# A fused attention and mixture-of-experts kernel: its general path moved into loops

## The chip, the cores and the metric

The kernel runs on one core of one Trainium2 chip. The metric is device time in microseconds, the median over runs. A profile is one execution, recorded by the hardware profiler; its span runs from the first to the last instruction.

## The reference

Two blocks follow each other. The first is attention with 8 batches, 8 heads, 576 positions and 64 values for each head, with a window of 128 positions and a bias that falls with distance. Its output is laid out as 4608 tokens of 512 values. The second sends each token to one of 8 experts:

```python
scores = np.where(mask, scale * (q @ k.T) + bias, -1e9)   # 0 <= i - j < 128
x = (softmax(scores) @ v)                                 # -> (4608, 512)
logits = x @ w_gate
expert_idx = np.argmax(logits, axis=1)
gate_w = softmax(logits)[np.arange(N), expert_idx]
for e in range(8):                                        # the tokens of expert e
    y[e's tokens] = np.maximum(x[e's tokens] @ w1[e], 0) @ w2[e]
out = gate_w[:, None] * y
```

The inputs are small random numbers (normal, times 0.1 or less).

## The kernel before

**Attention.** The 4608 tokens are 36 tiles of 128. A loop that is written out in full runs over 32 units, each two heads of one batch. For each unit TensorE forms scores (L639), ScalarE their exponentials (L646), VectorE multiplies with a table of distance factors (L652), and TensorE multiplies with the values (L672). This form takes no maximum before the exponential, so it is only right where the sums of exponentials stay in range.

**Routing.** While that runs, the logits of each tile give every token an expert and a slot. GpSimd scatters the rows of `x` to `x_rows`, a tensor in HBM with a region for each expert, with one indirect DMA for each tile (`scatter`, which calls `to_x_rows`, L135). `clear` writes rows of zeros behind an expert's last token with further indirect DMAs.

**Experts.** `experts(True)` takes each expert's first 512 rows in one full group, by seven products in place of eight (`seven1`, `seven2`, L1048), and between the full groups seven single tiles of 128 for what overflows the 512. `send_out` (L465) scatters each tile of results to the output with an indirect DMA on GpSimd. The order of instructions on each engine is the order of the text: the whole stretch stands under `tc.manual_schedule()`.

**The general path.** Three things can break the fast path: sums of exponentials out of range, more than seven overflowing tiles, and fewer than 256 early rows for the first expert. `count_in_range` and `what_is_left` count them on VectorE, behind the expert with index 1, into `n_more`. At the end one register tells whether any of them happened:

```python
    with tc.If(more[0] == 0, label="nothing", preferred_fallthrough_block=False) as nothing:
        pass
    with nothing.Else():
        n_bad = nc.values_load(n_more_i[0:1, 1:2], ...)
        with tc.If(n_bad > 0):
            n_pass[0] = 1
            shifted()
            clear(free_rows[:, 0, :])
            with moe_pools(), tc.manual_schedule():
                experts(False)
```

`shifted()` is attention once more, tile by tile and with a maximum; `experts(False)` is the whole of the experts once more, written out. Below it stand a short group for the early rows and a loop over further overflowing tiles. With the inputs here none of the three happens, and the branch "nothing" is taken.

**Semaphores across a branch.** Instructions signal semaphores that only count up, and later waits are for fixed counts. A branch that skips code therefore has to raise each semaphore by what the skipped code would have added. For the engines and for SP's DMAs this is one semaphore instruction each. For GpSimd's own DMAs, which take turns on eight semaphores DMASW0 to DMASW7 and add 16 each, it is one instruction with eight amounts, INC_SWDGE_SEM. These instructions stand in the block "nothing" and carry the line of the outer `tc.If` (L1268). The end of the program, with a DRAIN on each engine and barriers among all of them, carries the line that opens the tile context (L1316).

Of the kernel before, what the change touches and what calls it, by code (L numbers as in the profile page):

```python
# [8 lines left out]
F32 = mybir.dt.float32  # L9
# [6 lines left out]
P = 128  # L16
# [5 lines left out]
def kernel(  # L22
# [92 lines left out]
    RW = Dm + 2  # L115
    x_d = nc.dram_tensor("x_rows", (E * N, RW), F32, kind="Internal").ap()
    zero_row = consts.tile([P, RW], F32, name="zero_row")
    soon.append(lambda: nc.gpsimd.memset(zero_row[:], 0.0))
# [15 lines left out]
    def to_x_rows(row, numbers, apart=True):  # L134
        ins = nc.gpsimd.indirect_dma_start(  # L135
            out=x_d[:, :], out_offset=bass.IndirectOffsetOnAxis(ap=numbers, axis=0),
            in_=row, in_offset=None, bounds_check=E * N - 1, oob_is_err=False,
        )
        ins = getattr(ins, "ins", ins)
        if apart:  # L140
            tc.declare_no_dep(ins, group=f"rows_in{n_pass[0]}", reason="disjoint rows")
            tc.add_to_no_dep_group(f"rows_in{n_pass[0]}", ins)

# [11 lines left out]
    n_routed = [0]  # L155
    n_pass = [0]

# [96 lines left out]
    def shifted():  # L254
        with tc.tile_pool(name="bias", bufs=1) as b_pool, \
# [44 lines left out]
            for t in range(NT):  # L300
# [79 lines left out]
                nc.vector.tensor_scalar_add(gw[:], gw[:], 1e-9)  # L380
                if t == NT - 1:
                    number_all_free(rows)
                xs = rows.tile([P, RW], F32, name="xs")
                nc.scalar.copy(xs[:, :Dm], xf)
                nc.vector.tensor_copy(xs.bitcast(I32)[:, Dm : Dm + 1], tok_i[:, t : t + 1])
                nc.vector.reciprocal(xs[:, Dm + 1 :], gw[:])
                scatter(t, xs[:])

    xe = rte.tile([1, NX], I32, name="xe")
    n_more = rte.tile([1, 4], F32, name="n_more")
    n_more_i = rte.tile([1, 4], I32, name="n_more_i")
    xr = rte.tile([1, NX], I32, name="xr")
    xmasks = rte.tile([P, 2, NX], I32, name="xmasks")

    def extras(scr):
        used = [0]

        def part(rows, n, m=None):  # L400
# [3 lines left out]
            return t if m is None else t.rearrange("p (a b) -> p a b", b=m)  # L404


        def to_masks(out, has):
            nc.vector.tensor_scalar_mul(out[:, 0], has, -1.0)
            nc.vector.tensor_scalar(
                out[:, 1], has, scalar1=-float(2 * N), scalar2=float(2 * N), op0=ALU.mult, op1=ALU.add,  # L410
            )

# [51 lines left out]
    def send_out(g, j, row):  # L464
        ins = nc.gpsimd.indirect_dma_start(  # L465
            out=out[:, :], out_offset=bass.IndirectOffsetOnAxis(ap=g["si"][:, j : j + 1], axis=0),
            in_=row, in_offset=None, bounds_check=N - 1, oob_is_err=False,
        )
        ins = getattr(ins, "ins", ins)
        if g["apart"]:  # L470

            tc.declare_no_dep(ins, group=f"rows_out{n_pass[0]}", reason="disjoint rows")
            tc.add_to_no_dep_group(f"rows_out{n_pass[0]}", ins)

# [486 lines left out]

    def what_is_left(first):
        if first:
            gps = pools["ps"].tile([P, DB * P], F32, name="tp")
            nc.tensor.matmul(gps[:, 0:1], lhsT=ones_sq[:], rhs=n_in[:], start=True, stop=True)
            nc.vector.tensor_scalar(
                n_more[:, 1:2], gps[0:1, 0:1], scalar1=-1.0, scalar2=float(N * H), op0=ALU.mult, op1=ALU.add,
            )

            nc.vector.tensor_scalar(  # L970
                n_more[:, 3:4], early_n[0:1, :], scalar1=-1.0, scalar2=float(EJ * P), op0=ALU.mult, op1=ALU.add,
            )
            nc.vector.tensor_scalar_max(n_more[:, 3:4], n_more[:, 3:4], 0.0)

            nc.vector.tensor_scalar(
                n_more[:, 2:3], n_more[:, 0:1], scalar1=-float(XU), scalar2=0.0, op0=ALU.add, op1=ALU.max,
            )
            nc.vector.tensor_add(n_more[:, 2:3], n_more[:, 2:3], n_more[:, 1:2])
            nc.vector.tensor_add(n_more[:, 2:3], n_more[:, 2:3], n_more[:, 3:4])
        else:  # L980
            nc.vector.memset(n_more[:, 1:], 0.0)
        nc.vector.tensor_copy(n_more_i[:], n_more[:])
# [178 lines left out]

    def of_x(x):
        ex = nc.sync.value_load(xe[0:1, x], min_val=0, max_val=E - 1)
        return (
            moe_w1[bass.ds(ex, 1)].rearrange("e d f -> (e d) f"), moe_w2[bass.ds(ex, 1)].rearrange("e f d -> (e f) d"),
        )

    def rows_of_x(x):
        r0 = nc.sync.value_load(xr[0:1, x], min_val=0, max_val=E * N - P)
        return x_d[bass.ds(r0, P), :]  # L1170

    def get_w1(g):
        g["src"] = of_x(g["x"]) if "x" in g else (moe_w1[g["e"]], moe_w2[g["e"]])
        g["w1"] = load_w1(g["src"][0])
# [4 lines left out]

    def experts(first):  # L1180
        groups = []
        for e in range(E):

            j0 = EJ if first and e == 0 else 0
            groups.append(dict(
                n=NJ - j0, e=e, rows=lambda r=e * N + j0 * P, n=NJ - j0: x_d[r : r + n * P, :], apart=True,
            ))
            if e > 0:
                x = slice(e - 1, e)
                groups.append(dict(n=1, x=x, rows=lambda x=x: rows_of_x(x), mask=xmasks[:, :, x], apart=True))  # L1190
        g = groups[0]
        if first:
            g["w1"], g["w2"] = expert_w.pop(0)
        else:
            get_w1(g)
        gather(g)
        get_w1(groups[1])
        gather(groups[1])
        if not first:
            g["w2"] = load_w2(g["src"][1])  # L1200
            extras(pools["wk"].tile([P, FB, NJ * P], F32, name="h_sb").rearrange("p f n -> p (f n)"))
            run(w1_sums(g))
        turns = [lambda: turn(g, range(g["n"])), lambda: tokens(g)]
        if first:
            zx = pools["u"].tile([P, Dm], F32, name="zx", bufs=1)
            layer2(early, EJ - 1, bank(2), zx[:], between=turns)
        else:
            run(turns)
            x_sums(g)
        for i, g in enumerate(groups):  # L1210
# [6 lines left out]
            if g["n"] == NJ:  # L1217
                hidden(g)
                order = (1, 6, 7, 5, 2, 3, 4)
                ws = w2_sums(g)  # L1220
                seven1(g, 0, order, two_banks(3), temps(), {6: ws[:1], 7: ws[1:2], 5: ws[2:3], 3: ws[3:]})
                if i == 1:
                    what_is_left(first)
                seven1(g, 1, order, two_banks(3), temps(), {})
            else:
                if i == 0:
                    run(w1_sums(full[0]))
                for fb in range(FB):
                    layer1(g, fb, bank(fb))
            if after[1] is not None:  # L1230
                get_w1(after[1])
            if after[0] is not None:
                turn(after[0], range(after[0]["n"]))
                tokens(after[0])
                if after[0]["n"] == NJ:
                    x_sums(after[0])
            if i == 0 and first:
                count_in_range()
            if g["n"] == NJ:
                g["zo"] = pools["wk"].tile([P, NJ, Dm], F32, name="zo")  # L1240

                ws = w1_sums(full[0]) if full else []
                seven2(g, {5: ws[:1], 2: ws[1:2], 3: ws[2:3], 4: ws[3:]})
            else:
                plain_layer2(g, ahead=[is_there_more] if first and i == len(groups) - 1 else ())

# [5 lines left out]
    with moe_pools():  # L1252
        tc.mark_branch_hint_location("nothing", engines=mybir.ALL_ENGINES)
        experts(True)
    order_all.close()

    def plain_group(g):
# [7 lines left out]
        plain_layer2(g)  # L1265


    with tc.If(more[0] == 0, label="nothing", preferred_fallthrough_block=False) as nothing:  # L1268
        pass
    with nothing.Else():  # L1270
        n_bad = nc.values_load(n_more_i[0:1, 1:2], min_val=0, max_val=N * H)
        with tc.If(n_bad > 0):
            n_pass[0] = 1
            shifted()
            clear(free_rows[:, 0, :])
            with moe_pools(), tc.manual_schedule():
                experts(False)

        n_short = nc.values_load(n_more_i[0:1, 3:4], min_val=0, max_val=EJ * P)
        with tc.If(n_short > 0):  # L1280
            with moe_pools():
                plain_group(dict(n=EJ, e=0, rows=lambda: x_d[: EJ * P, :], apart=False))

        nx = nc.values_load(n_more_i[0:1, 0:1], min_val=0, max_val=NX)
        with tc.If(nx > XU):
            with moe_pools(), tc.For_i(XU, nx, 1) as i:
                mk = pools["u"].tile([P, 2, 1], I32, name="mk")
                nc.vector.tensor_copy(mk[:], xmasks[:, :, bass.ds(i, 1)])
                x = bass.ds(i, 1)
                plain_group(dict(n=1, x=x, rows=lambda: rows_of_x(x), mask=mk, apart=False))  # L1290

# [28 lines left out]
```

## Time and profile before

| | |
|---|---|
| median of 4 runs | 724.0 us |
| lowest and highest run | 722.19 and 726.42 us |
| profiled execution | 723.61 us, span 721.8 us |
| mean granted TensorE clock | 0.989 |
| instructions in the span | 13669 |
| GpSimd's indirect DMAs in the span | 107 (68 to `x_rows`, 39 to the output) |
| last matmul ends | about 706 us after the start |

Idle time of an engine that is not the bottleneck costs nothing. In the profile an engine's name with a q behind it is its sequencer, which reads instructions, branches and waits for semaphores; such instructions are not counted as busy. The length given for a DMA that GpSimd issues is the time GpSimd spends on it, not the time until its data has landed.

### The profile page before, as it was taken

How to read it: one execution, taken by the hardware profiler on the slowest of the kernel's cores; microseconds unless marked ns; L12 is line 12 of the kernel's file. 1: busy time of each engine (PE TensorE's matmuls, PEld its weight loads, DVE VectorE, ACT ScalarE, POOL GpSimd, SP SyncE). 2: the span in 40 equal slices, each digit the busy share in tenths (PEclk: the TensorE clock that was granted, in tenths of full speed). 3: DMA queues.
4: the chain of work that ended last, by engine and by line, in shares of the span. 5: the costliest groups of instructions: out<-in, count | busy, mean ns of one | idle time of the engine just before them, and what ended most of it. 6: DMA issues, size and time to landing. Idle time of an engine off the chain costs nothing.

```text
span 721.8 us, 13669 instructions
## 1 busy us (share of the span) xinstructions
PE 687.9 (95%) x5662; PEld 560.4 (78%) x5662; DVE 345.4 (48%) x705; ACT 215.6 (30%) x543; POOL 120.0 (17%) x146
## 2 busy tenths in 40 slices
PE   6999999999899999999999999999999999999991
PEld 5777677766676688878897887889788888978880
DVE  4577666675763354426335533634562463435300
ACT  5655455554411121222131212112121221212120
POOL 1011322023343020121022002202200220200020
PEclk9999999999999999999999999999999999999996
DMA  9966789852226736265353617534362735371010
GB/s 268 272 207 191 237 273 297 232 169 75 90 90 210 269 88 233 68 231 175 132 186 140 238 56 280 189 132 164 140 197 111 282 120 202 99 273 51 1 60 4
DMA packets 52722, 121.49 MB, mean 168 GB/s; under 512 B 7185, under 2 KB 7185, under 8 KB 52656
## 3 DMA queue, kind: packets, MB, share of 16 engines
q1 hardware_dynamic: 43568, 101.50, 43.0%
q0 software_dynamic: 8560, 19.06, 7.2%
q8 instruction: 45, 0.74, 0.4%
q14 instruction: 21, 0.17, 0.1%
q10 hardware_dynamic: 528, 0.02, 0.0%
HBM read 101.51 MB, written 28.12 MB: 180 GB/s over the span
## 4 chain that ended last, share of the span: by engine, by line
PE 82%; issue 11%; DVE 3%; POOL 1%; DMA 1%; ACT 0%; SPq 0%; POOLq 0%; DVEq 0%
PE b L1048 17%; PE a L1048 11%; PE c L1048 11%; PE sp L639 7%; PE m L672 7%; PE a L517 6%; PE sm L693 3%; PE b L506 3%; PE a L506 3%; PE m L804 2%; PE m L506 2%; PE c L506 2%; PE tp L497 1%; PE m L753 1%; PE c L517 1%
## 5 line engine op out<-in xcount | busy, mean ns | idle before, releaser
L465 POOL DMA_INDIRECT out_dram<-zo,si x28 | 29.6, 1059 | 292.8 <-ACT zo L1118 288.5
L646 ACT ACTIVATE e<-sp 128x384 f32<-128x384 f32 x128 | 55.7, 492 | 52.1 <-PE sp L639 24.0
L639 PE MATMUL sp<-q_sb,k_sb 64*64 64x192 f32 (+2 forms) x1152 | 58.8, 325 | 9.5 <-DMA k_sb<-in_kT_dram 5.4
L672 PE MATMUL m<-probs,v_sb 64*64 64x192 f32 (+2 forms) x1152 | 62.6, 316 | 5.3 <-issue 3.5
L672 PEld LDWEIGHTS m<-probs,v_sb 64*64 64x64 f32 x1152 | 53.3, 135 | 14.6 <-issue 8.2
L639 PEld LDWEIGHTS sp<-q_sb,k_sb 64*64 64x64 f32 x1152 | 47.8, 138 | 21.0 <-issue 10.1
L517 PE MATMUL a<-w,h 128*128 128x512 f32 x128 | 56.3, 592 | 0.0
L1118 ACT ACTIVATE zo<-zo,gw 128x256 f32<-128x256 f32 x42 | 19.1, 502 | 119.4 <-DVE zo L1129 78.2
L1048 PE MATMUL a<-xgT,w 128*128 128x256 f32 x224 | 53.0, 379 | 0.0
L1048 PE MATMUL b<-xTs,w1s 128*128 128x256 f32 x224 | 52.9, 379 | 0.0
L1048 PE MATMUL a<-w,h_sb 128*128 128x256 f32 x224 | 50.6, 379 | 0.0
L1048 PE MATMUL b<-w2s,hs 128*128 128x256 f32 x224 | 50.6, 379 | 0.0
L1048 PEld LDWEIGHTS a<-xgT,w 128*128 128x128 f32 x224 | 42.5, 190 | 8.7 <-issue 3.3
L1048 PEld LDWEIGHTS b<-xTs,w1s 128*128 128x128 f32 x224 | 42.6, 190 | 5.8
L1048 PEld LDWEIGHTS b<-w2s,hs 128*128 128x128 f32 x224 | 42.6, 190 | 5.8
L1048 PEld LDWEIGHTS a<-w,h_sb 128*128 128x128 f32 x224 | 42.0, 190 | 5.4
L652 DVE TENSOR_TENSOR probs<-e,fac 128x1152 f32<-128x1152 f32 x32 | 43.3, 1352 | 3.0 <-ACT e L646 3.0
L517 PEld LDWEIGHTS a<-w,h 128*128 128x128 f32 x128 | 23.7, 190 | 26.8 <-issue 26.8
L135 POOL DMA_INDIRECT x_rows<-xs,slots x36 | 38.0, 1055 | 15.2 <-POOL xs L820 6.4
L1078 DVE TENSOR_TENSOR u<-b,p 128x512 f32<-128x512 f32 x14 | 9.7, 692 | 56.6 <-PE b L1048 28.7
L1082 ACT ACTIVATE h_sb<-h_sb 128x512 f32<-128x512 f32 x14 | 8.8, 631 | 84.3 <-DVE h_sb L1081 84.3
L681 DVE TENSOR_TENSOR xT<-xT,m 128x128 f32<-128x128 f32 x32 | 9.1, 284 | 51.1 <-ACT xT L680 51.1
(246 smaller groups left out, 1152.0 us busy)
## 6 DMA issues: line engine op xcount, KB each, us to landing
w<-in_moe_w_dram SPq DMA_DIRECT2D x28, 2048.0 KB
q_sb<-in_qT_dram SPq DMA_DIRECT2D x32, 288.0 KB
k_sb<-in_kT_dram SPq DMA_DIRECT2D x32, 288.0 KB
xg<-x_rows SPq DMA_DIRECT2D x16, 514.0 KB
v_sb<-in_v_dram SPq DMA_DIRECT2D x24, 256.0 KB
w<-in_moe_w_dram SPq DMA_DIRECT2D x8, 512.0 KB
v_sb<-in_v_dram SPq DMA_DIRECT2D x24, 128.0 KB
xg<-x_rows SPq DMA_DIRECT2D x7, 257.0 KB
```

What stands on the lines that cost most here:

```text
L135: ins = nc.gpsimd.indirect_dma_start(out=x_d[:, :], out_offset=bass.IndirectOffsetOnAxis(ap=numbers, axis=0), in_=row, in_offset=None, bou ...
L465: ins = nc.gpsimd.indirect_dma_start(out=out[:, :], out_offset=bass.IndirectOffsetOnAxis(ap=g["si"][:, j : j + 1], axis=0), in_=row, in_of ...
L506: nc.tensor.matmul(ps[:, :n], lhsT=g["w1"][:, db, fb * P : (fb + 1) * P], rhs=g["xT"][:, db, :n], start=(db == 0), stop=(db == DB - 1),)
L517: nc.tensor.matmul(ps[:], lhsT=g["h"][:, fb, j * P : (j + 1) * P], rhs=g["w2"][:, fb, :], start=(fb == 0), stop=(fb == FB - 1),)
L639: nc.tensor.matmul(sp_banks[2 * par + s][r * HALF : (r + 1) * HALF, c : c + n], lhsT=k_sb[u][head, k0 : k0 + HALF], rhs=q_sb[u][head, q0 : ...
L646: nc.scalar.activation(exps[u][:, c], sp_banks[s][:, : W // 2], AF.Exp, scale=D ** -0.5)
L652: nc.vector.tensor_tensor(to[:, :, : 3 * C].rearrange("p a (j c) -> p a j c", c=C), e[:, :, : 3 * C].rearrange("p a (j c) -> p a j c", c=C ...
L672: nc.tensor.matmul(xp[r][par * HALF : (par + 1) * HALF, q0 : q0 + n], lhsT=v_sb[b][keys, i, h * D : (h + 1) * D], rhs=probs[u][keys, par, ...
L693: nc.tensor.matmul(sm[g : g + 32, i * HALF : i * HALF + C], lhsT=one_c[:, hp, :], rhs=probs[u][:, par, c : c + C], start=(hp == 0 and i == ...
L804: nc.tensor.transpose(m[:, 2 * hp : 2 * hp + 2, :].rearrange("p h d -> p (h d)"), xT[pair][:, hp, c : c + P], ident[:],)
L1048: nc.tensor.matmul(out_of[:, i, :], lhsT=lhs(i, k), rhs=rhs(k), start=(first and i == 0 and k == 0), stop=(k == nk - 1), skip_group_check= ...
L1118: nc.scalar.activation(o[:, th, dh, i, :], src[:, i, :], AF.Copy, scale=g["gw"][:, j : j + 1])
```

## The change

In the general path, `shifted()` no longer scatters its 36 tiles of rows with 36 indirect DMAs that are written out. It stores each tile to a new tensor `x_by_token` with a plain DMA, and a loop then loads tile after tile and scatters it with the one indirect DMA in its body. `experts(False)` is gone: a second loop takes the 32 tiles (8 experts of 4) one by one, with masks in place of rows of zeros. The loop over overflowing tiles is shared as `one_tile`; its first index becomes a fifth value in `n_more`. `experts` loses its argument, and the groups of declared independence their pass number.

```diff
+    x_tok = nc.dram_tensor("x_by_token", (NT, P, RW), F32, kind="Internal").ap()
...
@@ shifted
-                if t == NT - 1:
-                    number_all_free(rows)
...
-                scatter(t, xs[:])
+                nc.sync.dma_start(x_tok[t], xs[:])
...
-    n_more = rte.tile([1, 4], F32, name="n_more")
-    n_more_i = rte.tile([1, 4], I32, name="n_more_i")
+    n_more = rte.tile([1, 5], F32, name="n_more")
+    n_more_i = rte.tile([1, 5], I32, name="n_more_i")
...
@@ what_is_left
+        nc.vector.memset(n_more[:, 4:5], float(XU))
...
+    def one_tile(i, of, first_row, masks):
+        mk = pools["u"].tile([P, 2, 1], I32, name="mk")
+        nc.vector.tensor_copy(mk[:], masks[:, :, bass.ds(i, 1)])
+        x = bass.ds(i, 1)
+        plain_group(dict(
+            n=1, of=lambda: of_x(x, of), rows=lambda: rows_of_x(x, first_row), mask=mk, apart=False,
+        ))
+
+    def all_again():
+        shifted()
+        with tc.tile_pool(name="again", bufs=1) as again:
+            with tc.For_i(0, NT, 1) as i:
+                xs = again.tile([P, RW], F32, name="xs")
+                sl = again.tile([P, 1], I32, name="sl")
+                nc.sync.dma_start(xs[:], x_tok[bass.ds(i, 1)].rearrange("o p r -> (o p) r"))
+                nc.vector.tensor_copy(sl[:], slots[:, bass.ds(i, 1)])
+                to_x_rows(xs[:], sl[:], False)
+            extras(again.tile([P, FB * NJ * P], F32, name="scr"))
...
+            with moe_pools(), tc.For_i(0, E * NJ, 1) as i:
+                one_tile(i, fe.rearrange("o e j -> o (e j)"), fr.rearrange("o e j -> o (e j)"), fmasks)
...
+        nc.vector.memset(n_more[:, 1:], 0.0)
+        nc.vector.tensor_copy(n_more_i[:], n_more[:])
...
         with tc.If(n_bad > 0):
-            n_pass[0] = 1
-            shifted()
-            clear(free_rows[:, 0, :])
-            with moe_pools(), tc.manual_schedule():
-                experts(False)
+            all_again()
...
+        x0 = nc.values_load(n_more_i[0:1, 4:5], min_val=0, max_val=XU)
         nx = nc.values_load(n_more_i[0:1, 0:1], min_val=0, max_val=NX)
-        with tc.If(nx > XU):
-            with moe_pools(), tc.For_i(XU, nx, 1) as i:
-                ...
+        with tc.If(nx > x0):
+            with moe_pools(), tc.For_i(x0, nx, 1) as i:
+                one_tile(i, xe, xr, xmasks)
```

More of the change, by code (lines that the diff above doesn't have):

```diff
@@ L140, in to_x_rows @@
         if apart:
-            tc.declare_no_dep(ins, group=f"rows_in{n_pass[0]}", reason="disjoint rows")
-            tc.add_to_no_dep_group(f"rows_in{n_pass[0]}", ins)
+            tc.declare_no_dep(ins, group="rows_in", reason="disjoint rows")
+            tc.add_to_no_dep_group("rows_in", ins)
     def clear(rows, apart=True):
@@ L155 @@
     n_routed = [0]
-    n_pass = [0]
     early_end = (NB - 2) * S // P
@@ L386, in shifted, with to_masks @@
                 nc.vector.reciprocal(xs[:, Dm + 1 :], gw[:])
-                scatter(t, xs[:])
+                nc.sync.dma_start(x_tok[t], xs[:])
     xe = rte.tile([1, NX], I32, name="xe")
-    n_more = rte.tile([1, 4], F32, name="n_more")
-    n_more_i = rte.tile([1, 4], I32, name="n_more_i")
+    n_more = rte.tile([1, 5], F32, name="n_more")
+    n_more_i = rte.tile([1, 5], I32, name="n_more_i")
     xr = rte.tile([1, NX], I32, name="xr")
     xmasks = rte.tile([P, 2, NX], I32, name="xmasks")
+    def to_masks(out, has):
+        nc.vector.tensor_scalar_mul(out[:, 0], has, -1.0)
+        nc.vector.tensor_scalar(
+            out[:, 1], has, scalar1=-float(2 * N), scalar2=float(2 * N), op0=ALU.mult, op1=ALU.add,
+        )
     def extras(scr):
@@ L404, in part @@
             return t if m is None else t.rearrange("p (a b) -> p a b", b=m)
[L407 to L411, printed above, removed]
         og = part(P, E, NX)
@@ L470, in send_out @@
         if g["apart"]:
-            tc.declare_no_dep(ins, group=f"rows_out{n_pass[0]}", reason="disjoint rows")
-            tc.add_to_no_dep_group(f"rows_out{n_pass[0]}", ins)
+            tc.declare_no_dep(ins, group="rows_out", reason="disjoint rows")
+            tc.add_to_no_dep_group("rows_out", ins)
     def tokens(g):
@@ L960, in count_in_range, with what_is_left @@
         nc.vector.reduce_sum(n_in[:], inr, axis=AX)
[L962 to L981, printed above, removed]
+    def what_is_left():
+        gps = pools["ps"].tile([P, DB * P], F32, name="tp")
+        nc.tensor.matmul(gps[:, 0:1], lhsT=ones_sq[:], rhs=n_in[:], start=True, stop=True)
+        nc.vector.tensor_scalar(
+            n_more[:, 1:2], gps[0:1, 0:1], scalar1=-1.0, scalar2=float(N * H), op0=ALU.mult, op1=ALU.add,
+        )
+        nc.vector.tensor_scalar(
+            n_more[:, 3:4], early_n[0:1, :], scalar1=-1.0, scalar2=float(EJ * P), op0=ALU.mult, op1=ALU.add,
+        )
+        nc.vector.tensor_scalar_max(n_more[:, 3:4], n_more[:, 3:4], 0.0)
+        nc.vector.memset(n_more[:, 4:5], float(XU))
+        nc.vector.tensor_scalar(
+            n_more[:, 2:3], n_more[:, 0:1], scalar1=-float(XU), scalar2=0.0, op0=ALU.add, op1=ALU.max,
+        )
+        nc.vector.tensor_add(n_more[:, 2:3], n_more[:, 2:3], n_more[:, 1:2])
+        nc.vector.tensor_add(n_more[:, 2:3], n_more[:, 2:3], n_more[:, 3:4])
         nc.vector.tensor_copy(n_more_i[:], n_more[:])
@@ L1160, in hidden, with of_x @@
         g["hs"] = pools["wk"].tile([P, 4, FH, TH], F32, name="hs")
-    def of_x(x):
-        ex = nc.sync.value_load(xe[0:1, x], min_val=0, max_val=E - 1)
+    def of_x(x, of=xe):
+        ex = nc.sync.value_load(of[0:1, x], min_val=0, max_val=E - 1)
         return (
@@ L1166, in of_x, with rows_of_x @@
         )
-    def rows_of_x(x):
-        r0 = nc.sync.value_load(xr[0:1, x], min_val=0, max_val=E * N - P)
+    def rows_of_x(x, of=xr):
+        r0 = nc.sync.value_load(of[0:1, x], min_val=0, max_val=E * N - P)
         return x_d[bass.ds(r0, P), :]
     def get_w1(g):
-        g["src"] = of_x(g["x"]) if "x" in g else (moe_w1[g["e"]], moe_w2[g["e"]])
+        g["src"] = g["of"]() if "of" in g else (moe_w1[g["e"]], moe_w2[g["e"]])
         g["w1"] = load_w1(g["src"][0])
@@ L1178, in plain_layer2, with experts @@
             layer2(g, j, bank(j), pools["u"].tile([P, Dm], F32, name="zx", bufs=1)[:], ahead=ahead)
-    def experts(first):
+    def experts():
         groups = []
         for e in range(E):
-            j0 = EJ if first and e == 0 else 0
+            j0 = EJ if e == 0 else 0
             groups.append(dict(
@@ L1189, in experts @@
                 x = slice(e - 1, e)
-                groups.append(dict(n=1, x=x, rows=lambda x=x: rows_of_x(x), mask=xmasks[:, :, x], apart=True))
+                groups.append(dict(
+                    n=1, of=lambda x=x: of_x(x), rows=lambda x=x: rows_of_x(x), mask=xmasks[:, :, x], apart=True,
+                ))
         g = groups[0]
[L1192 to L1195, printed above, removed]
+        g["w1"], g["w2"] = expert_w.pop(0)
         gather(g)
@@ L1198, in experts @@
         gather(groups[1])
[L1199 to L1202, printed above, removed]
+        zx = pools["u"].tile([P, Dm], F32, name="zx", bufs=1)
         turns = [lambda: turn(g, range(g["n"])), lambda: tokens(g)]
[L1204 to L1209, printed above, removed]
+        layer2(early, EJ - 1, bank(2), zx[:], between=turns)
         for i, g in enumerate(groups):
@@ L1222, in experts @@
                 if i == 1:
-                    what_is_left(first)
+                    what_is_left()
                 seven1(g, 1, order, two_banks(3), temps(), {})
@@ L1236, in experts @@
                     x_sums(after[0])
-            if i == 0 and first:
+            if i == 0:
                 count_in_range()
@@ L1244, in experts @@
             else:
-                plain_layer2(g, ahead=[is_there_more] if first and i == len(groups) - 1 else ())
+                plain_layer2(g, ahead=[is_there_more] if i == len(groups) - 1 else ())
     more = []
@@ L1253 @@
         tc.mark_branch_hint_location("nothing", engines=mybir.ALL_ENGINES)
-        experts(True)
+        experts()
     order_all.close()
@@ L1265, in plain_group @@
         plain_layer2(g)
+    def one_tile(i, of, first_row, masks):
[4 more added lines that the diff above has]
+            n=1, of=lambda: of_x(x, of), rows=lambda: rows_of_x(x, first_row), mask=mk, apart=False,
+        ))
+    def all_again():
[8 more added lines that the diff above has]
+            extras(again.tile([P, FB * NJ * P], F32, name="scr"))
+            fe = again.tile([1, E, NJ], I32, name="fe")
+            fr = again.tile([1, E, NJ], I32, name="fr")
+            fmasks = again.tile([P, 2, E * NJ], I32, name="fmasks")
+            has = again.tile([P, E, NJ], F32, name="has")
+            nc.gpsimd.iota(fe[:], pattern=[[1, E], [0, NJ]], base=0, channel_multiplier=0)
+            nc.gpsimd.iota(fr[:], pattern=[[N, E], [P, NJ]], base=0, channel_multiplier=0)
+            nc.vector.tensor_tensor(
+                has[:], cnt[:].unsqueeze(2).to_broadcast([P, E, NJ]), tail[:, None, :].to_broadcast([P, E, NJ]),
+                op=ALU.is_gt,
+            )
+            to_masks(fmasks, has.rearrange("p e j -> p (e j)"))
+            with moe_pools(), tc.For_i(0, E * NJ, 1) as i:
+                one_tile(i, fe.rearrange("o e j -> o (e j)"), fr.rearrange("o e j -> o (e j)"), fmasks)
+        nc.vector.memset(n_more[:, 1:], 0.0)
+        nc.vector.tensor_copy(n_more_i[:], n_more[:])
     with tc.If(more[0] == 0, label="nothing", preferred_fallthrough_block=False) as nothing:
@@ L1282 @@
                 plain_group(dict(n=EJ, e=0, rows=lambda: x_d[: EJ * P, :], apart=False))
+        x0 = nc.values_load(n_more_i[0:1, 4:5], min_val=0, max_val=XU)
         nx = nc.values_load(n_more_i[0:1, 0:1], min_val=0, max_val=NX)
-        with tc.If(nx > XU):
-            with moe_pools(), tc.For_i(XU, nx, 1) as i:
[L1287 to L1290, printed above, removed]
+        with tc.If(nx > x0):
+            with moe_pools(), tc.For_i(x0, nx, 1) as i:
+                one_tile(i, xe, xr, xmasks)
 def kernel(q, k, v, moe_w_gate, moe_w1, moe_w2):
```

## The prediction

> **What bounds the kernel now.** I first read the busy table, the slices and the windows, to see which stages the change could reach. The first row is the page's busy table; the row of slices shows PE in fortieths of the span; the windows give microseconds, busy time and instructions of each engine.
>
> ```profile
> PE 687.9 (95%) x5662; PEld 560.4 (78%) x5662; DVE 345.4 (48%) x705; ACT 215.6 (30%) x543; POOL 120.0 (17%) x146
> ...
> PE   6999999999899999999999999999999999999991
> ...
> 690.00:708.20 18.20, 16.22 (x91) 11.79 (x89) 0.69 (x1) 4.12 (x13) 4.89 (x5) 1.00 0.16 60
> 708.20:722.00 13.80, 0.00 (x0) 0.00 (x0) 0.00 (x0) 0.00 (x0) 0.00 (x1) 0.56 0.01 4
> ```
>
> TensorE bounds everything up to the last matmul. After the last scatter's issue come 13.6 us of span (708.2 to 721.8) in which no engine computes. Next I asked for the instructions of the two lines that stand there: L1268 is the outer `tc.If`, L1316 the end of the program. Columns: engine, where q is its sequencer; operation; count; minimum, median and maximum in ns; first and last start.
>
> ```profile
> L1268 POOLq EVENT_SEMAPHORE  x6: 17/30/1780, 707.5 to 709.7; - x6
> L1268 POOLq COMPARE_BRANCH  x1: 70/70/70, 707.0 to 707.0; - x1
> L1268 POOLq INC_SWDGE_SEM  x1: 2336/2336/2336, 709.8 to 709.8; - x1
> ...
> L1316 POOLq DRAIN  x3: 40/109/8807, 712.1 to 721.5; - x3
> L1316 SPq DRAIN  x3: 7/7/13, 712.8 to 721.2; - x3
> ```
>
> The tail is one chain on GpSimd: branch at 707.0, a wait of 1.78 us, a raise of semaphores of 2.34 us from 709.8, a DRAIN of 8.81 us from 712.1 to 720.9, and 0.9 us of barriers. The wait is for the last scatter, from the timeline:
>
> ```profile
> 707.22 0.98 POOL L465 DMA_INDIRECT out_dram<-zx,si  x1 [11.21 <-ACT zx L521]
> ```
>
> **The general path itself: nothing.** The trace takes the "nothing" branch: after L1268 no matmul runs. So neither the 36 stores of `x_tok` nor the loop over 32 tiles nor a loop's barriers is ever issued. In the built programs the instructions up to the branch stand in the same order on all five engines, with the same waits, and the SBUF addresses of their tiles agree. One instruction is added: DVE's memset of `n_more[:, 4:5]`. Its price is that of the nearest row, 59 ns (MEMSET one_c 64x1); the copy of five values for four costs nothing I can see beside its 157 ns. Behind it on DVE stands `u<-b,p` at 272.11, 0.69 long. PE writes bank b again only at 273.25, 0.45 us after that ends, so 0.06 us is hidden; with that cover gone it would be 0.06 us, once. In HBM `x_rows` keeps its place; the new tensor lies behind it.
>
> **The tail: the raise.** When the branch skips the general path, each semaphore of GpSimd's DMAs must be lifted by what the skipped code would have added, 16 for each DMA in the text of the program. Before, that text holds 36 scatters, 32 zero rows and 39 output scatters in `experts(False)`, 2 in the short group and 1 in the loop: 110, spread over all eight semaphores. After, a loop's body counts once: 1 scatter, 1 tile, 2 short, 1 more, so 5, on five semaphores. In the built program of before the raise waits for all eight; in that of after, for DMASW3 to DMASW7. The last scatter signals DMASW2. So the 1.78 us wait for its landing leaves the raise's way: that is the one move on a path that sets the end.
>
> Now the sum. In the trace GpSimd's six semaphore instructions start at 707.5 and come about 0.1 us apart; with two fewer waits, all of them long satisfied, the raise can start at about 707.9. If it must first see the scatter's descriptors written, it starts at 708.2 (707.22 + 0.98). I take the middle, 708.05. Its duration has one row of this kind, 2336 ns for eight semaphores. Upper bound: the same. By share of semaphores, 5/8: 1.46. Lowest: the 31 ns of the empty instruction of the same name at the program's start. I take 2.0, nearest to the only row of this mode. The raise then ends at 710.05 instead of 712.1. The scatter has landed by 709.6, where the 1.78 us wait ends, so the DRAIN finds it done: it moves earlier by 2.05 us whole.
>
> Bounds of this term: raise at 708.2 and still 2.34 long, 710.54, saves 1.6; raise of 1.46 from 707.9 saves 2.7; a raise of almost nothing at 707.9 lets the DRAIN begin at 707.95 and saves 4.2, if the DRAIN can work through older DMAs while the last one lands. Below: if the raise internally waits for every DMA of the queue, it starts at 709.7 and saves 0.1. Less than nothing only comes from the last rival.
>
> **The tail: the DRAIN.** Its 8807 ns is the largest piece, and the trace has it once. Two counts fit equally well. DMAs that GpSimd ran: 36 + 28 + 2 + 2 to x_rows and 28 + 10 + 1 to the output, from the list of DMA issues, make 107, or 82 ns each. DMAs that it skipped: 110, or 80 ns each. The first count does not change, the second falls to 5. I take the first: SP's waits for the eight raised values start at 712.1 and its own DRAIN follows at 712.8, so the raised values are posted before GpSimd's DRAIN has run a tenth of its time, and nothing of the skip seems left to do; the 107 DMAs did go through GpSimd. If the second holds, the DRAIN falls to 5 x 80 = 0.4 us, a gain of 8.4.
>
> [...]
>
> **The sum.** The profiled execution took 723.61 us, 1.8 outside its span, and stands 0.4 below the median of 724.0. 723.61 - 2.05 + 0 = 721.6; on the median, 721.9. About 0.5% (3.6 us) is what a measurement of this kernel can tell from no change, with runs from 722.2 to 726.4; 2.05 us is 0.3% and lies within it.
>
> **Rivals.**
>
> *The DRAIN goes with what is skipped* (29%). For: 80 ns each is as round as 82, and the eight semaphores that were lifted out of band belong to the very queue that is drained. Against: the raised values are posted before it works. 723.61 - 2.05 - 8.4 = 713.2, on the median 713.5. A half-way form, the DRAIN by raised semaphores (8.8 x 5/8 = 5.5), gives 718.6.
>
> *Nothing moves* (7%): the raise sees to the whole queue, the waits or not. 0.1 us: 723.9. The text's fewer instructions help nobody, since they were never run.
>
> *Slower: a fetch at the branch* (6%). Place: GpSimd, between the branch at 707.0 and the raise. The blocks "nothing" and end lie at other distances than before. The page's queue of instructions gives the price:
>
> ```profile
> q8 instruction: 45, 0.74, 0.4%
> ```
>
> 0.4% of 16 x 721.8 us over 45 packets is 1.0 us each; one packet took 2.2. Against: before, GpSimd goes from branch to next instruction in 0.4 us across a longer gap. If both blocks have to be fetched at 2.2 each, the raise starts at 711.9 and ends at 714.2, 2.1 late: 726.1. It decides from about 2 us of fetching on, where it eats the gain, and passes 0.5% from 5.7 us on, three such packets. The Trainium skill (Runtime: NRT & Kernel Launch, section "Instruction fetch mechanics") speaks for this one: a taken branch to a place outside the pages at hand stalls for a fetch. By it the distance makes no difference, since both programs jump; by the row, it cost 0.4 us.
>
> **How the numbers follow.** The likeliest case, the raise moved and the DRAIN as long, has 58%; its own range is 719.8 (saving 4.2) to 723.9. Of it 12 lie beyond 0.5% (a short raise and the spread of the runs). Faster: 12 + 29 = 41%. Within: 46 of it, 7 of nothing moved and 3 of the fetch, 56%. Slower: the fetch's other 3%. For 8 in 10 the range must take in the drain's rival: from 713.0, just below its 713.5, to 723.9; what is left out is the fetch, a part of nothing moved and the spread of the runs below 713.0.
>
> **What would show it.** Right: the page's rows of L1292 and L1334 (the two lines' new numbers) have INC_SWDGE_SEM starting near 708 instead of 709.8, lasting 1.5 to 2.3 us, DRAIN still near 8.8, and the stage to 708.2 unchanged to 0.3 us. A DRAIN of under 1 us makes the first rival right; one near 5.5, its half-way form. A raise still at 709.8 is the second; a gap over 1 us behind the branch the third. A difference that lies before 707 would make the whole account wrong.

## The result, and the profile after

The changed kernel takes 722.81 us (median of 52 runs) where the kernel before takes 723.7 us (median of 78 runs): ratio 0.9986, 95% interval 0.9975 to 0.9996. By the ratio that is 1.0 us (the medians differ by 0.9), below the 0.5% that the prediction takes as the bound of no change, though the interval lies just under 1. The forecast was 721.9 us, 713.0 to 723.9. The profiled execution took 723.12 us, with a span of 721.4 us.

First the rows of the two lines that stand in the tail of the kernel after, L1292 (the outer `tc.If`) and L1334 (the end of the program); the columns are those of the rows shown before the change.

```profile
L1292 POOLq EVENT_SEMAPHORE  x4: 17/30/43, 709.0 to 709.3; - x4
L1292 POOLq COMPARE_BRANCH  x1: 70/70/70, 708.5 to 708.5; - x1
L1292 POOLq INC_SWDGE_SEM  x1: 2346/2346/2346, 709.4 to 709.4; - x1
...
L1334 POOLq DRAIN  x3: 40/109/8807, 711.7 to 721.1; - x3
L1334 SPq DRAIN  x3: 7/7/13, 712.4 to 720.8; - x3
```

Two of the six semaphore instructions are gone, and with them the wait of 1780 ns: the longest that is left takes 43 ns. The raise keeps its length (2346 ns, before 2336) and the DRAIN keeps its length to the nanosecond (8807). The starts have to be read against the last scatter, which the timeline has here:

```profile
708.70 0.98 POOL L463 DMA_INDIRECT out_dram<-zx,si  x1 [11.21 <-ACT zx L519]
```

Before, it started at 707.22. From the scatter's start the raise now begins after 0.66 us in place of 2.55, and the span ends after 12.7 us in place of 14.6. The tail is 1.9 us shorter. In these two executions most of that is hidden, because the scatter itself came 1.48 us later. The same stretches as before, from the windows of the kernel after:

```profile
690.00:708.20 18.20, 17.70 (x98) 13.09 (x96) 1.38 (x2) 4.36 (x13) 3.91 (x4) 1.00 0.16 59
708.20:722.00 13.80, 0.00 (x0) 0.00 (x0) 0.00 (x0) 0.23 (x1) 0.98 (x1) 0.61 0.02 5
```

TensorE is busy 17.70 us instead of 16.22 in the first stretch: the same work, 1.48 us later. Where that delay arose is told by a landmark in the middle, TensorE's first group of `seven1` into bank b. From the timeline of the kernel before, and then of the kernel after:

```profile
257.49 1.89 PE L1048 MATMUL b<-xTs,w1s 128*128 128x256 f32 x8
```

```profile
258.97 1.89 PE L1044 MATMUL b<-xTs,w1s 128*128 128x256 f32 x8
```

From the landmark to the last scatter it is 449.73 us in both, and the added memset lies in that stretch (273.00 in the trace after). The memset costs nothing; the whole 1.48 us lies ahead of 257.5 us, where the change adds no instruction. There the granted clock differs. In the windows the third column from the end is that clock; the stretch is 34.13 us long, and a halved clock for 3.4 us, the unit in which the trace records it, takes 0.05 off the mean (in finer windows the kernel before has 0.50 from 129.71 to 133.12 and 1.00 around it). Before, after, and the run `e2_early_drain` told of below:

```profile
102.40:136.53 34.13, 30.92 (x547) 23.42 (x543) 20.84 (x57) 17.25 (x51) 6.09 (x9) 0.95 0.95 277
```

```profile
102.40:136.53 34.13, 30.86 (x513) 23.48 (x514) 20.80 (x57) 15.74 (x47) 6.57 (x10) 0.90 0.92 285
```

```profile
102.40:136.53 34.13, 31.25 (x559) 23.99 (x559) 21.90 (x56) 18.34 (x58) 5.57 (x8) 1.00 1.02 284
```

One such unit in the first, two in the second, none in the third, and TensorE gets through 547, 513 and 559 matmuls. Over all eleven traces of this study the landmark tends to come later with more half-clock units ahead of it: none, 255.96 us; one, 256.0 to 258.0; two, 257.1 to 259.3; three, 259.0 and 260.2; five, 262.65. The clock is not the whole of it: half the clock for 3.4 us can cost 1.7 us at most (an estimate from these rows), and the run at 258.0 with one unit is 2.0 us behind the one with none. The stretch from the landmark to the last scatter is 449.73 us in every one of them. So all tails below are measured from the last scatter's start.

### The profile page after: what moved, and what is told of

Read it like the earlier page. It is cut to its first block, busy times and chain, and to the rows that moved or that the text cites. A ratio compares the mean times of both kernels' runs of the same rounds, so it can differ in the third digit from the quotient of the medians.

```text
span 721.4 us, 13668 instructions
## 1 busy us (share of the span) xinstructions
PE 688.4 (95%) x5662; PEld 560.8 (78%) x5662; DVE 345.4 (48%) x706; ACT 215.2 (30%) x543; POOL 119.9 (17%) x146
## 4 chain that ended last, share of the span: by engine, by line
PE 80%; issue 12%; DVE 4%; SPq 1%; POOL 1%; DMA 1%; ACT 0%; POOLq 0%; DVEq 0%
PE b L1044 17%; PE a L1044 12%; PE c L1044 11%; PE m L670 7%; PE a L515 6%; PE sp L637 6%; PE sm L691 3%; PE b L504 3%; PE a L504 3%; PE m L802 2%; PE m L504 2%; PE c L504 2%; PE tp L495 1%; DVE probs L650 1%; PE m L751 1%
## 5 line engine op out<-in xcount | busy, mean ns | idle before, releaser
L670 PE MATMUL m<-probs,v_sb 64*64 64x192 f32 (+2 forms) x1152 | 65.3, 319 | 8.0 <-issue 6.1
L637 PE MATMUL sp<-q_sb,k_sb 64*64 64x192 f32 (+2 forms) x1152 | 56.3, 320 | 8.0 <-DMA k_sb<-in_kT_dram 5.3
## 6 DMA issues: line engine op xcount, KB each, us to landing
v_sb<-in_v_dram SPq DMA_DIRECT2D x24, 256.0 KB
```

The source lines that it names most:

```text
L637: nc.tensor.matmul(sp_banks[2 * par + s][r * HALF : (r + 1) * HALF, c : c + n], lhsT=k_sb[u][head, k0 : k0 + HALF], rhs=q_sb[u][head, q0 : ...
L670: nc.tensor.matmul(xp[r][par * HALF : (par + 1) * HALF, q0 : q0 + n], lhsT=v_sb[b][keys, i, h * D : (h + 1) * D], rhs=probs[u][keys, par, ...
```

## Experiments

Theory: the raise left the landing wait, and the lengths of the raise and of the DRAIN come from the DMAs that GpSimd ran (a DMA is called open until a DRAIN has gone through it). Rivals: the lengths go with what the branch skips; or the raise's own length depends on how many semaphores it lifts and by how much. All tails in one table; "open" counts the run DMAs since the last DRAIN.

| kernel | open | raise starts, us after the scatter | raise, ns | last DRAIN, ns | scatter to end, us |
|---|---|---|---|---|---|
| before | 107 | 2.55 | 2336 | 8807 | 14.6 |
| after | 107 | 0.66 | 2346 | 8807 | 12.7 |
| e1_all_eight | 107 | 2.55 | 2336 | 8807 | 14.6 |
| e7_fast_path_part | 107 | 2.55 | 2336 | 8807 | 14.6 |
| e9_four_more_dmas | 111 | 0.66 | 2442 | 9134 | 13.1 |
| e4_eight_more_dmas | 115 run | 0.66 | 386 | 1724 | 4.0 |
| e8_half_open | 51 | 0.66 | 1226 | 4223 | 7.0 |
| e2_early_drain | 1 | 0.66 | 209 | 1569 | 4.0 |
| e3_before_early_drain | 1 | 2.55 | 199 | 140 | 4.35 |
| e6_no_general_path | 107 | no raise | - | 10025, from before the scatter | 10.6 |

**Give the wait back.** Eight indirect DMAs are added to the general path, where they are never run, so that the raise again has an amount for each of the eight semaphores. The changed kernel runs again beside it.

```diff
         shifted()
+        clear(free_rows[:, 0, :], False)
+        clear(free_rows[:, 1, :], False)
         with tc.tile_pool(name="again", bufs=1) as again:
```

> The changed kernel with eight more indirect DMAs in the text of the general path, which is never run, so that the branch has to raise all eight semaphores again; the loops, the shorter text and the fast path stay as changed. Theory (the gain is the moved raise alone): the raise starts after the last scatter has landed, 2.4 to 2.6 us after GpSimd took the scatter up instead of 0.66; it lasts 2.3 us as in both kernels although the amounts are now 16 and 32 instead of 208 and 224; the DRAIN stays at 8.81; from the scatter to the end 14.5 us as before the change, and the time is that of before, 1.000. Rival (the loops or the shorter text give the gain): from the scatter to the end stays at 12.7 and the ratio at 0.9985. Rival (the raise costs by its amounts): the raise falls to about 0.5 us.

> The changed kernel unaltered, beside the others on one chip. Theory: from the last scatter to the end 12.7 us against 14.56, the fast path equal, so a ratio of 0.9974. Rival (something in the changed program makes the fast path longer and gives half of it back): a ratio of 0.9985 to 0.999 here, and at the same time a ratio of 1.001 for the kernel that raises all eight semaphores.

With the eight: 725.6 us, ratio to before 1.0017 (0.9994 to 1.004). Without: 722.4 us, ratio 0.9986 (0.9963 to 1.0009). The rows of the run with the eight:

```profile
L1294 POOLq EVENT_SEMAPHORE  x6: 17/30/1779, 710.2 to 712.4; - x6
L1294 POOLq INC_SWDGE_SEM  x1: 2336/2336/2336, 712.5 to 712.5; - x1
...
L1336 POOLq DRAIN  x3: 40/109/8807, 714.9 to 724.3; - x3
```

Six semaphore instructions and the wait of 1.78 us are back, and with them the old tail. That the raise waited for the landing was worth 1.9 us, and nothing else in the changed general path was worth anything in the tail. The raise took 2336 ns for 13 skipped DMAs as for 110, so its length goes neither with their number nor, but for 10 ns, with the number of semaphores.

The rows settle the tail; the whole time they do not settle. The two ratios, 0.9986 and 1.0017, fit what the second text's rival named (a fast path that became longer: 0.9985 to 0.999, and 1.001), while the theory's 0.9974 and 1.000 lie inside both intervals.

**Close the older DMAs early.** One DRAIN of GpSimd ahead of the last scatter, first in the changed kernel, later in the kernel before.

```diff
-                plain_layer2(g, ahead=[is_there_more] if i == len(groups) - 1 else ())
+                plain_layer2(g, ahead=[nc.gpsimd.drain, is_there_more] if i == len(groups) - 1 else ())
```

> The changed kernel with one more DRAIN on GpSimd, placed between the last scatter but one and the last, where GpSimd is idle for 11.2 us. Theory (a DRAIN takes 82 ns for each DMA that GpSimd has run and that no earlier DRAIN has closed): the early DRAIN takes 1.5 us for the landing of the scatter before it at most and 106 x 82 ns = 8.7 us of work, and ends at about 705 to 706, before the last scatter at 707; the DRAIN at the end has one DMA left and ends within 0.3 us of its landing; if the raise walks the open DMAs too it falls to about 0.4 us, else it stays at 2.34; the stretch from the scatter to the end falls from 12.7 to 3.4 to 4.2 us and the time by about 9 us, a ratio to before of 0.985. Rival (the 8.8 us are a fixed price of a DRAIN after a raise, or of the program's end): the last DRAIN stays at 8.8 and the time is that of the changed kernel or longer.

Measured: 713.2 us, ratio to before 0.986 (0.9828 to 0.9892). The early DRAIN and the rows of the tail:

```profile
L525 POOLq DRAIN  x1: 10630/10630/10630, 692.6 to 692.6; - x1
```

```profile
693.51 0.98 POOL L463 DMA_INDIRECT out_dram<-zo,si  x1 [0.30 <-issue]
705.69 0.98 POOL L463 DMA_INDIRECT out_dram<-zx,si  x1 [11.20 <-ACT zx L519]
```

```profile
L1292 POOLq INC_SWDGE_SEM  x1: 209/209/209, 706.4 to 706.4; - x1
...
L1334 POOLq DRAIN  x3: 46/115/1569, 706.6 to 709.4; - x3
```

The DRAIN's record starts on the sequencer while the scatter ahead of it, at 693.51, is still to come; from the end of that issue, 694.5, to 703.2 it closes the 106 older DMAs, in 8.7 us of GpSimd's idle gap, 2.5 us before the last scatter starts at 705.69. What is left at the end is one open DMA: the raise falls to a tenth, and the final DRAIN ends 2.5 us after the scatter's start, about where the wait for the landing ended in the kernel before (2.4). The skipped DMAs are the same five as in the kernel after, so neither length is theirs.

> The kernel before with one DRAIN of GpSimd ahead of its last scatter, as the run with the early DRAIN had it in the changed kernel. Theory (the change moves only the raise out of the landing wait; the lengths of the raise and of the final DRAIN come from the GpSimd DMAs that are still open, run ones alone): the raise starts 2.55 us after the scatter as in the kernel before and takes 0.2 us in place of 2.34, the final DRAIN has nothing left to wait for and takes 0.05 to 0.2 us in place of 8.81, the same barriers of 0.9 us follow: 3.7 to 3.9 us from the scatter's start to the end in place of 14.56. That is no more than the 4.0 us of the changed kernel with the early DRAIN, since the landing ends last in both: the change's gain is gone, and the ratio to the kernel before is 0.985. Rival (the 110 skipped DMAs of the general path have a part in the two): the raise or the DRAIN stays longer than in the changed kernel by the share that belongs to them, up to 4 us in all.

Measured: 712.1 us, ratio 0.9829 (0.9804 to 0.9854).

```profile
L1268 POOLq EVENT_SEMAPHORE  x6: 17/30/1787, 712.6 to 714.8; - x6
L1268 POOLq INC_SWDGE_SEM  x1: 199/199/199, 714.9 to 714.9; - x1
...
L1316 SPq EVENT_SEMAPHORE  x14: 17/28/28, 715.1 to 716.7; - x14
L1316 POOLq DRAIN  x3: 46/109/140, 715.2 to 716.5; - x3
```

The wait for the landing is there (1787 ns), all 110 DMAs are skipped, and raise and DRAIN are 199 and 140 ns. The skipped DMAs have no part in either. The tail is 4.35 us, not the 3.7 to 3.9 that I expected: SP's row of 14 short waits only starts at 715.1, behind the raise, and the barrier comes after it. With the queue closed early, the change is worth 0.4 us of tail: both versions then wait for the same landing. With the run of eight more DMAs below, these are the fastest versions here; their ratios (0.986, 0.9829 and 0.9852) do not tell them apart.

**Half of the DMAs open.** The same DRAIN, but near 309 us, ahead of the first extra tile's scatter; 51 of the 107 follow it.

```diff
-                plain_layer2(g, ahead=[is_there_more] if i == len(groups) - 1 else ())
+                plain_layer2(g, ahead=[nc.gpsimd.drain] if i == 2 else [is_there_more] if i == len(groups) - 1 else ())
```

> The changed kernel with one DRAIN of GpSimd ahead of the first extra tile's scatter (near 323 us, in a gap of 12.8 us of GpSimd), so that 51 of the 107 run DMAs are still open at the end. Theory (cost in proportion to the open DMAs): early DRAIN 56 x 82 = 4.6 us inside the gap; raise 0.21 + 50 x 0.0202 = 1.2 us; final DRAIN 51 x 82 = 4.2 us, up to 4.7 if it also waits out the rest of the landing; 7.3 to 7.8 us from the scatter to the end in place of 12.7, ratio to the kernel before 0.990. Rival (a fixed price that is paid once the count passes some bound, not one for each DMA): raise 2.3 or 0.2, DRAIN 8.8 or 1.6.

Measured: 718.1 us, ratio 0.9912 (0.9878 to 0.9945).

```profile
309.74 0.98 POOL L463 DMA_INDIRECT out_dram<-zo,si  x1 [0.30 <-ACT h L508]
```

```profile
L525 POOLq DRAIN  x1: 8662/8662/8662, 308.6 to 308.6; - x1
...
L1292 POOLq INC_SWDGE_SEM  x1: 1226/1226/1226, 709.7 to 709.7; - x1
...
L1334 POOLq DRAIN  x3: 46/109/4223, 710.9 to 715.7; - x3
```

Each open DMA costs the raise (2346 - 1226) / 56 = 20.0 ns and the DRAIN (8807 - 4223) / 56 = 81.9 ns. A fixed price is ruled out. Two things did not fit. The tail is 7.0 us, a little under the 7.3 to 7.8 expected. And the early DRAIN closed its 56 DMAs in 6.6 us from the end of the last issue ahead of it (310.72), not in 4.6. Why stays open; it lay in an idle gap. The price of 81.9 ns is thus that of the DRAINs at the end, and of the early ones just ahead of the last scatter (106 in 8.7 us).

**More DMAs.** Eight, then four more executed scatters, of the zero rows of experts 3 and 4 (or 3 alone), to a spare tensor.

```diff
             clear(free_rows[:, g["e"], :])
+            if g["e"] in (3, 4):
+                for j in range(NJ):
+                    nc.gpsimd.indirect_dma_start(out=spare[:, :], in_=zero_row[:], ...)
```

> The changed kernel with eight more indirect DMAs that are run in the fast path (the zero rows of experts 3 and 4 written a second time, to a spare tensor that nobody reads), 115 instead of 107. Theory (82 ns for each DMA run): the DRAIN at the end takes 115 x 82.3 = 9.47 us, 0.66 more, and the time rises by as much. Rival (by what was skipped, which is unchanged at 5, or fixed): 8.81. If the queue has to close older DMAs earlier because it is full, the DRAIN stays below 9.47 and single DMAs get longer than 0.98 us.

Measured, in two runs: 712.9 us, ratio 0.9852 (0.9807 to 0.9896). More DMAs made the kernel faster, and the tail fell to 4.0 us:

```profile
L1300 POOLq INC_SWDGE_SEM  x1: 386/386/386, 708.4 to 708.4; - x1
...
L1342 POOLq DRAIN  x3: 40/109/1724, 708.8 to 711.4; - x3
```

The timeline of GpSimd tells where the rest went. First the last three scatters of this run, then the two of the kernel after to compare:

```profile
694.25 0.98 POOL L464 DMA_INDIRECT out_dram<-zo,si  x1 [1.19 <-ACT zo L1115]
697.43 0.99 POOL L464 DMA_INDIRECT out_dram<-zo,si  x1 [2.19 <-ACT h L509]
707.72 0.98 POOL L464 DMA_INDIRECT out_dram<-zx,si  x1 [9.30 <-ACT zx L520]
```

```profile
695.24 0.98 POOL L463 DMA_INDIRECT out_dram<-zo,si  x1 [1.19 <-ACT zo L1114]
696.52 0.98 POOL L463 DMA_INDIRECT out_dram<-zo,si  x1 [0.31 <-issue]
```

The 114th DMA starts 3.18 us after the 113th; in the kernel after the same two are 1.28 apart. The row names ScalarE for the wait, but the ScalarE work that writes this scatter's rows had ended at 694.38. A raise of 386 ns is (386 - 209) / 20 = 9 open DMAs more than one. Most of the older DMAs had been closed by then, and the late start marks where. That a full queue closes older ones is my reading of it; the run with four more bounds the place. If it is so, about 105 DMAs were closed in the 2.2 us ahead of the 114th, some 21 ns each, a quarter of a DRAIN's price (an estimate from these rows). The last DRAIN's 1724 ns do not count the open ones, since it ends 2.8 us after the scatter's start, behind the landing.

> The changed kernel with 4 more executed scatters (the zero rows of expert 3, to a spare tensor): 111 run DMAs in place of 107, none of them delayed by a full queue. Theory (20.0 ns of the raise and 81.9 ns of the final DRAIN for each open DMA, from the runs with 51 and 107 open, and a queue that holds between 111 and 113): raise 2346 + 4 x 20.0 = 2426 ns, final DRAIN 8807 + 4 x 81.9 = 9134 ns, 13.1 us from the last scatter's start to the end in place of 12.7, and the last five scatters at the distances of the changed kernel (1.3, 2.2, 1.3, 12.2 us). Rival (the queue's bound lies lower, or closing goes by another count): raise under 0.5 and DRAIN under 2 us, as with eight more, and one of the last scatters late by 1.9 us.

```profile
L1300 POOLq INC_SWDGE_SEM  x1: 2442/2442/2442, 707.5 to 707.5; - x1
...
L1342 POOLq DRAIN  x3: 40/109/9134, 710.0 to 719.7; - x3
```

The DRAIN is 9134 ns, as worked out from the other two points; the raise is 16 ns over its sum. At 111 nothing is closed early (721.66 us, one run); at 115 it happened between the 113th and the 114th.

**No general path.** Branch and general path are left out of the changed kernel.

> The changed kernel without the general path and without its branch (left out: all work for inputs that the fast path cannot finish). No raise is left, so the final DRAIN can start as soon as the last scatter is issued, 1.0 to 1.1 us after its start. If the DRAIN closes the older DMAs while the last one lands: 107 x 82 ns = 8.8 us counted from there, and 0.9 to 1.2 us of barriers, 10.7 to 11.1 us from the scatter to the end (after: 12.7). If it must see the last landing, 2.4 us after the start, before it closes any: 12.1 to 12.4 us. Ratio to the kernel before 0.995 or 0.997, if the fast path is of the same length. If the raise closes nothing and were only moved beside the landing, leaving it out gains nothing over the changed kernel's tail: 12.7 us or more.

Measured: 718.3 us, ratio 0.9929 (0.9901 to 0.9957). The tail is 10.6 us, just under the 10.7 to 11.1 of a DRAIN that works beside the landing.

```profile
705.73 0.98 POOL L463 DMA_INDIRECT out_dram<-zx,si  x1 [11.20 <-ACT zx L519]
```

```profile
L1315 POOLq DRAIN  x3: 40/107/10025, 705.5 to 716.1; - x3
```

The first DRAIN starts ahead of the scatter on GpSimd's sequencer and ends at 715.52. The scatter's issue ends at 705.73 + 0.98 = 706.71, and 8.81 us later is 715.52: the DRAIN works through the older DMAs while the last one is still landing. The 2.1 us that the kernel after pays above this are its raise, which does nothing of the DRAIN's work.

**The fast path's part alone.** The kernel before with `n_more` of five columns and the memset.

```diff
-    n_more = rte.tile([1, 4], F32, name="n_more")
+    n_more = rte.tile([1, 5], F32, name="n_more")
...
+            nc.vector.memset(n_more[:, 4:5], float(XU))
```

> The kernel before with the fast path's part of the change alone: n_more of five columns and the memset of 59 ns; the general path is the old one, with its 110 skipped DMAs. Theory: the tail is that of the kernel before (14.56 us, raise after the landing), the memset is covered, ratio 1.000, within 0.002. Rival (the fast path became longer by some 0.8 us, which is why the medians moved by 1.0 us and not by the tail's 1.85): ratio 1.001 or more.

Measured: 725.1 us, ratio 1.0007 (0.9982 to 1.0031), an interval that holds the rival's 1.001 too. The tail is that of before, and the stretch from the landmark to the last scatter is 449.73 us again, memset and all. The ratio alone could not have told 0.8 us from nothing; the stretch does, for everything behind 257 us.

## Why the prediction was right

**The mechanism was the one predicted.** That the time lies in the range shows little: the range runs from 713.0 to 723.9, and the kernel before lies in it with 723.7. The rows of the tail show it. The raise no longer waits for the last scatter, and a wait was all that was removed. `e1_all_eight` put it back with amounts for skipped DMAs alone, and the old tail with it.

**Start of the raise.** Predicted 0.83 us after the scatter's start (708.05 against 707.22), measured 0.66, just under the lower bound of 0.68: it does not wait for the end of the scatter's issue (0.98 us). In the run with the early DRAIN, where it takes 209 ns, it has even ended before that, 0.87 us after the scatter's start.

**Length of the raise, the term that was mis-sized.** Taken as 2.0 us between 0.03, 1.46 and 2.34; measured 2.35. The share by semaphores (5/8) was wrong, and so was any scale in what is skipped: it goes with open DMAs at 20.0 ns each, which the change leaves alone. The plain reading, that the one row of this kind stays as it is, would have been right. Start and length together: 2.05 us predicted, 1.9 measured. That the sum is so near is in part luck: the start was 0.17 us earlier and the length 0.35 us longer than taken, and the two errors pull in opposite directions.

**The DRAIN.** Two counts fitted one row, 107 x 82 ns and 110 x 80 ns, and the text chose the first. The runs with 51 and 111 open give 81.9 ns for each run DMA, and with 110 skipped and one open it takes 140 ns. The rival that had 29% is refuted, with its half-way form. The argument used for the choice (the raised values are posted before the DRAIN has worked) was sound but thin; a choice by the text alone could not have had much more than the odds that it was given.

**How long a DRAIN is.** The Trainium skill (VectorE: DVE Perf Modes, section "The DRAIN you can't avoid") puts the DRAINs that the runtime adds before and after a kernel at about 12 ns, constant, on all five engines. The traces here show only DRAINs of the program itself, so none of them tests that figure. It must not be carried over to them: SP's took 7 to 13 ns at the end of the program, but GpSimd's longest took 140, 4223, 8807 and 9134 ns with 1, 51, 107 and 111 open DMAs.

**Nothing moves, and the fetch at the branch.** The raise did not see to the landing on its own, so the second rival falls. From the start of the branch to the first semaphore instruction it is 0.5 us in both traces (707.0 to 707.5, 708.5 to 709.0): no fetch of a packet's length showed. Both kernels give a hint for this branch (`tc.mark_branch_hint_location("nothing", ...)`; the traces have a BRANCH_PREFETCH_HINT on each engine 0.8 us after the start); what the same branch costs without the hint no run here shows.

**What was to show it.** INC_SWDGE_SEM near 708, relative to the scatter, and a DRAIN near 8.8: right; 1.5 to 2.3 us for the raise missed by 0.05. The stage up to 708.2 was to be unchanged to 0.3 us, and a difference before 707 was to make the whole account wrong. That test was badly made: there is a difference of 1.48 us before 707, and by itself it says nothing about the change, because the landmark of single executions differs by more than that: 255.96 to 260.24 us over five traces (`after`, `after_again`, e1, e2, e8) whose code ahead of it is the same. The test should have been on distances from the last scatter.

**What stays open.** The time moved by 1.0 us by the ratio, the tail by 1.9. In us the interval of the ratio is 0.3 to 1.8 us (of 723.7), so it just misses 1.9. From the landmark on there is no room for a loss. Whether the part ahead of it is a little longer in the changed kernel, or the runs happened to fall so, no run here settles.

## What to carry to other kernels

When a change touches code that is skipped, look at what the skip itself does on the path: which semaphores it must raise, and what those waits have ahead of them. Here GpSimd's DRAIN at the end had a price for each indirect DMA that GpSimd had run since the last one. With a DRAIN of that engine in an idle gap shortly before its last DMA the bill was paid beside other work: it took 8.7 us off the tail of the changed kernel and 10.2 us off that of the kernel before. Measure tails from a landmark close to them, not from the start of the span.

## What the runs showed of the hardware that was not expected

- GpSimd's DRAIN at the end takes about 0.05 us and 81.9 ns for each open indirect DMA (4223, 8807 and 9134 ns with 51, 107 and 111), also when all of them have landed: in the kernel before it starts 2.5 us after the wait for the last landing has ended. It can work while the last one lands (10025 ns in the run without a raise). Each of these DMAs names 128 rows, so a price for each DMA and one for each row are not told apart.
- The raise of the DMA semaphores (INC_SWDGE_SEM) takes about 0.2 us and 20.0 ns for each further open DMA (209, 1226, 2346 and 2442 ns with 1, 51, 107 and 111), whatever it raises, and starts while the last scatter's issue is still running.
- With 115 executed DMAs the 114th came 1.9 us late, and the raise at the end was that of about ten open DMAs, not of 115.
- In the eleven traces the clock ahead of 257 us is halved for none to five stretches of 3.4 us. The landmark there came between 255.96 us (none) and 262.65 us (five), and the 449.73 us behind it stayed the same.
